# Attention and gated MLP on one core: another way to store the softmax sums, another planner model, another set of priorities

## The chip, the cores and the metric

The kernel runs on one core of a Trainium2 chip. The metric is the device time in microseconds (us) of one execution. TensorE multiplies matrices, VectorE (DVE in the profile), ScalarE (ACT) and GpSimd (POOL) work on elements, and SyncE (SP) does nothing but issue the transfers (DMAs) in the order in which the program lists them.

## The reference

For 8 batches and 8 heads, with 576 positions and 64 columns a head, in float32:

```python
q_rot, k_rot = (rotate(q), rotate(k))                 # rotary embedding
scores = np.matmul(q_rot, k_rot.transpose(0, 1, 3, 2)) / np.sqrt(D)
attn = np.exp(scores - np.max(scores, axis=-1, keepdims=True))
attn = attn / (np.sum(attn, axis=-1, keepdims=True) + 1e-09)
x = np.matmul(attn, v)                                # heads joined: B, 576, 512
h = np.maximum(x @ w_in, 0.0)                         # 576 x 1024
u, v = (h[..., :512], h[..., 512:])
v_n = (v - mean(v)) / np.sqrt(var(v) + 1e-06)
v_s = np.einsum('ts,bsd->btd', w_spatial, v_n) + b_spatial[None, :, None]
out = (u * v_s) @ w_out
```

## The kernel before

**Tiles.** Two heads of a batch are one pair; there are 32 pairs, numbered `i`, four to a batch. Of a pair, `prepare` loads q and k (`st`, L549), turns them by the rotary table (`rope` L541, `rope_sum` L545, mostly on POOL), splits them into a high and a low part (L557 on ACT, L532 on DVE, L422 for the low parts) and copies them into the stacks that TensorE reads (`stk`, L568 to L575, ten DMAs a pair). `scores` (L782) makes nine score tiles of 128 x 576; `soften` takes the row maximum (L825, DVE), the exponential with its row sums (L828, ACT) and, from the fifth pair on, a 32 x 32 block transposition (L830, DVE). The product with the values, the "v product" (L741), comes in two halves of 144 matmuls each in the profile; each half is 288 instructions with its weight loads. The first four pairs (`i < PLAIN`) take another path, with transpositions on TensorE (L664, L667) and wider v products (L710).

**The sums.** `normalise` turns the nine columns of row sums into reciprocals (L862), transposes the 128 x 32 tile in 32 x 32 blocks (`rt`, L863), so that in each of the four 32-partition groups ("quadrants") the rows hold the sums of 32 positions, and stores them to DRAM: `put`, eight DMAs for the first four pairs, six for the others. `get` reads them back, spread over 64 partitions for each head (`rb`, two DMAs), L867 multiplies, and L419 and L422 split the product `x` into its parts for the MLP.

**The MLP** of a batch (`mlp`) needs the four `x` of the batch. Its products, in order: `rows` (L901, the only ones 512 columns wide, here called wide products), u (L924), the spatial ones (L942) and the output (L957), all the last three 288 columns wide. The weights come as pairs of 32-bit words and are decoded on DVE, ACT and POOL (`decode`) in the early part of the run.

**The order.** The kernel's instructions are not issued in the order of the text. Each piece of work is an `Op` with a modelled duration, a priority (`key`, a due time worked out from the pair's number and the constants `K_...`, `DEC_...`) and its dependences. `Program.run` simulates the five engines and the DMA queue with heaps: whenever an engine is free in the model, the ready op with the smallest key that finds its buffers is issued on it. The result is a fixed order for each engine; on the chip each engine follows its own in order and waits where an operand is late. For TensorE the model also has the arrival of instructions (`Feed`, L126): 256 of them come by one fetch, and an op of more than 200 instructions (only the halves of the v product) is put off while the model says that it would stall by over `STALL` ns (L267). In the model a finished op releases its followers `LATENCY` ns after its end; TensorE's own followers too, after 200 ns, though they run on the same engine.

```python
if item[2].count > 200 and item is not dense and feed.walk(now, item[2].costs[e], item[2].count, wire, False) > STALL:
```

Of the kernel before, what the change touches and what calls it, by code (L numbers as in the profile page):

```python
# [31 lines left out]
TO_PE = 104  # L32
LATE = 1244
AHEAD = 1564
BATCH, AHEAD_OF, IN_FLIGHT = 256, 32, 8
FIRST = 1100
FETCH_MIN, FETCH_END, FETCH_LANE, SLOW, STALL = 1456, 2550, 830, 1800, 187
SLOTS = {
    "stage": 3, "lk": 1, "vrep": 1, "et": 2, "x32": 1, "xg": 7, "m": 4,
    "stk": 3, "small": 3, "nmx": 3, "rt": 2, "sc": 2, "pm": 4, "eh": 6,  # L40
# [3 lines left out]
DEC_V = [27.3, 49.5, 63.4, 71.3]  # L44
DEC_S = [38.0, 28.4, 82.6]
DEC_U = [67.4, 109.3, 103.5, 96.2]
DEC_O = [126.8, 108.3, 154.4, 146.7]
# [14 lines left out]
VALUES_AT2 = [17.2, 29.1]  # L62
K_HI, K_MUL, K_HALF = 0.94, 2.63, 5.44
# [11 lines left out]
K_TAIL = -17.27  # L75
K_INV, K_GET, K_X, K_XHI, K_XLO = 20.09, 69.48, 32.23, 48.57, 37.32
K_NORM, K_RELU, K_GATE, K_GHI, K_GLO, K_OB, K_OUT = 0.84, -5.79, -15.46, 19.4, -3.72, 0.16, 33.12
# [41 lines left out]
class Op:  # L119
    def __init__(self, costs, key, f, new, port):  # L120
        self.costs, self.key, self.f, self.new, self.port = costs, key, f, new, port
        self.eng, self.late, self.reserve, self.count = None, 0, False, 0
        self.waits, self.after, self.bufs = 0, [], []
# [27 lines left out]
class Program:  # L151
# [32 lines left out]
    def run(self, make):  # L184
# [45 lines left out]
        wire, feed, lands = 0, Feed(), [0] * IN_FLIGHT  # L230
# [4 lines left out]
        while events:  # L235
            now = events[0][0]
            while events and events[0][0] == now:
                _, _, what, o = heapq.heappop(events)
                if what == "ready":
                    for n_e, e in enumerate(o.costs):  # L240
                        heapq.heappush(ready[e], (o.key + STEAL * n_e, index[o], o))
                elif what == "free":
# [3 lines left out]
                else:  # L246
# [6 lines left out]
                    for a in o.after:  # L253
                        a.waits -= 1
                        if not a.waits:
                            late = TO_PE if PE in a.costs and o.eng != PE else 0
                            heapq.heappush(events, (now + late, n, "ready", a))
                            n += 1
            for e in LATENCY:
# [3 lines left out]
                while (ready[e] or dense) and not chosen:  # L263
# [25 lines left out]
                if chosen:  # L289
# [18 lines left out]
                    else:  # L308
                        gap = chosen.costs[e]
                        if e == PE:  # L310
                            gap += feed.walk(now, gap, chosen.count, wire, True)
                            end = now + gap
                    heapq.heappush(events, (now + gap, n, "free", e))
                    heapq.heappush(events, (end + LATENCY[e] + chosen.late, n + 1, "done", chosen))
                    n += 2
# [5 lines left out]
def tile_attention_gated_mlp(  # L321
# [21 lines left out]
    def T(shape, dt, name):  # L343
        return sb.tile(shape, dt, tag=name, name=name, bufs=1)

    def make(b):
# [6 lines left out]
        if b.pool == "rt":  # L353
            b.scratch = dr.tile([2, 5, P], F32, tag=tag, name=b.name + "d", bufs=1)
# [19 lines left out]
    sums = [T([P, 32], F32, f"sums{i}") for i in range(2)]  # L374
    wsp = T([P, 4, 2, S], F32R, "wsp")
# [141 lines left out]
    def prepare(i):  # L517
# [46 lines left out]
        for a in range(2):  # L564
# [3 lines left out]
            for dst, rows, part, tok, dep in (  # L568
# [6 lines left out]
                op(DMA, dma_ns(132, 1, 570, 2.9), key - (K_STACK2 if a else K_STACK), copy, r=[dep], w=[tok])  # L575
# [144 lines left out]
    def attention(i):  # L720
# [24 lines left out]
        o = op(PE, 2600, key + K_AV, lambda: multiply(0, half), r=need, w=pv, new=pv, count=32 * half)  # L745
        o.reserve = True
        op(PE, 2600, key + K_AV, lambda: multiply(half, NB), r=need, w=pv, count=32 * half)
# [84 lines left out]
    def normalise(i, sm, x32, key):  # L832
        rt = Buf("rt", [P, 32], F32, f"rt{i}")
# [4 lines left out]

        def put():
            main = rt.scratch[:, :4, :]  # L840
            for j in range(4):
                load(main[:, :, 32 * j:32 * j + 32], rt[32 * j:32 * j + 8, :])
            ends = rt.scratch[:, 4, :64]
            if i < PLAIN:
                for h in range(2):
                    for j in range(2):
                        load(ends[h:h + 1, 32 * j:32 * j + 32], rt[64 * h + 32 * j + 8:64 * h + 32 * j + 9, :])
            else:
                for h in range(2):
                    load(ends[h].rearrange("(g k) -> g k", g=4), rt.tile.rearrange("(g r) n -> g r n", r=32)[:, 8, 16 * h:16 * h + 16])  # L850

        def get():
            for h in range(2):
                row = rt.scratch[h].rearrange("t p -> (t p)").rearrange("(o n) -> o n", o=1)
                load(rb[64 * h:64 * h + 64, :], row[:, :S].to_broadcast([64, S]))
# [7 lines left out]
        op(DVE, 125, key + K_INV, lambda: nc.vector.transpose(out=rt.tile, in_=sm), r=need, w=[rt], new=[rt])  # L863
        op(DMA, dma_ns(5, 8 if i < PLAIN else 6, 330, 120), key + K_INV, put, r=[rt], w=[(rt, 1)])
        op(DMA, dma_ns(288, 2, 590, 5.2), key + K_GET, get, r=[(rt, 1)], w=[rb, "rbs"], new=[rb])
# [6 lines left out]
    def mlp(b):  # L872
# [6 lines left out]
        def mm(ns, f, each=HALF, **kw):  # L879
            key = base + MOE_LENGTH * spent[0] / whole  # L880
            spent[0] += ns
            op(PE, ns, key, f, count=2 * round(ns / pe_ns(each)), **kw)
# [220 lines left out]
```

## Time and profile before

| | |
|---|---|
| median of 3 runs | 846.47 us (839.14, 846.47, 847.57) |
| profiled execution | 843.61 us, of which the span from first to last instruction is 841.8 us |
| TensorE busy | 807.4 us, 96% of the span |
| DVE, ACT, POOL busy | 586.9, 527.2, 527.4 us |
| mean granted TensorE clock | 0.996 of full speed |
| DMA issues on SP | 778 |

In the profile PE is TensorE's matmuls and PEld its weight loads. An idle time is put down to the instruction whose semaphore came last; "issue" stands where the engine waited for nothing that the profile shows. The ends of matmuls are modelled, so that time in which they run slowly counts as busy.

### The profile page before, as it was taken

The page shows a single profiled execution, that of the slowest core. Times are in us where ns is not written, and L with a number is a line of the kernel's source. Part 1 is how long each engine was busy: PE and PEld are TensorE (multiplying, and loading weights), DVE is VectorE, ACT ScalarE, POOL GpSimd, SP SyncE. Part 2 cuts the span into 40 slices and gives each one's busy share as a digit, 9 for nine tenths or more (in the row PEclk, how much of TensorE's full clock was granted, in tenths as well). Part 3 has the DMA queues.
Part 4 walks back from the last instruction along what each step waited for, and adds up shares of the span by engine and source line. Part 5 has one row for each costly group of instructions (what it writes and reads, how often), then busy time and mean ns, then how long its engine had stood idle before and what let it go on. Part 6 is the DMA issues. An engine that isn't in the chain of part 4 may idle for free.

```text
span 841.8 us, 30199 instructions
## 1 busy us (share of the span) xinstructions
PE 807.4 (96%) x12560; PEld 725.6 (86%) x12560; DVE 586.9 (70%) x1172; ACT 527.2 (63%) x1378; POOL 527.4 (63%) x441
## 2 busy tenths in 40 slices
PE   5999889999999999999999999999999989999998
PEld 3556678998999988998888989998899988999898
DVE  6988987866987667676875678666587766765220
ACT  4889767565865558465764568655595555744442
POOL 5999587675758758486764758575566865423221
PEclk9999999999999999999999999999999999999999
DMA  9855666678777884778657688777757887373101
GB/s 330 295 176 139 164 177 150 176 184 218 174 188 199 193 226 131 167 182 244 168 143 190 168 198 202 180 187 187 196 145 175 216 209 178 73 166 76 44 2 57
DMA packets 63867, 144.56 MB, mean 172 GB/s; under 512 B 10993, under 2 KB 12785, under 8 KB 63730
## 3 DMA queue, kind: packets, MB, share of 16 engines
q1 hardware_dynamic: 63730, 142.63, 65.4%
q8 instruction: 99, 1.62, 0.8%
q14 instruction: 38, 0.31, 0.1%
HBM read 93.55 MB, written 9.58 MB: 123 GB/s over the span
## 4 chain that ended last, share of the span: by engine, by line
PE 75%; POOL 5%; DMA 5%; ACT 5%; DVE 4%; issue 3%; SPq 3%; POOLq 0%; DVEq 0%; ACTq 0%
PE psum L741 14%; PE psum L782 13%; PE psum L942 13%; PE psum L901 11%; PE psum L924 10%; PE psum L957 8%; SPq L416 3%; ACT et L828 2%; PE psum L802 2%; POOL st L541 2%; PE psum L710 1%; DMA st<-in_qk_dram 1%; DVE nmx L825 1%; POOL st L545 1%; PE psum L664 1%
## 5 line engine op out<-in xcount | busy, mean ns | idle before, releaser
L828 ACT ACTIVATE et<-psum,nmx 128x576 f32<-128x576 f32 x288 | 212.5, 740 | 125.4 <-DVE nmx L825 123.9
L825 DVE TENSOR_REDUCE nmx<-psum 128x1 f32<-128x576 f32 x288 | 210.7, 742 | 85.1 <-PE psum L782 77.4
L830 DVE STREAM_TRANSPOSE et<-et 128x576 f32<-128x576 f32 x252 | 192.4, 769 | 50.7 <-ACT et L828 49.6
L541 POOL TENSOR_TENSOR st<-st,tabs 128x576 f32<-128x576 f32 x112 | 164.2, 1479 | 59.1 <-DMA st<-in_qk_dram 33.5
L741 PE MATMUL psum<-et,vr 32*64 32x144 f32 x8064 | 147.0, 286 | 6.8 <-issue 2.9
L741 PEld LDWEIGHTS psum<-et,vr 32*64 32x64 f32 x8064 | 128.9, 130 | 21.8 <-issue 15.0
L942 PE MATMUL psum<-wsp,vn 128*128 128x288 f32 x768 | 124.9, 296 | 0.9 <-issue 0.9
L924 PE MATMUL psum<-x,wi 128*128 128x288 f32 x768 | 118.5, 296 | 2.4 <-issue 1.4
L901 PE MATMUL psum<-wi,x 128*128 128x512 f32 x448 | 118.6, 402 | 0.3 <-DVE sgwo L466 0.2
L957 PE MATMUL psum<-g,wo 128*128 128x288 f32 x768 | 118.2, 298 | 0.3 <-POOL g L422 0.2
L924 PEld LDWEIGHTS psum<-x,wi 128*128 128x128 f32 x768 | 108.0, 188 | 6.0 <-issue 4.0
L942 PEld LDWEIGHTS psum<-wsp,vn 128*128 128x128 f32 x768 | 109.4, 188 | 2.5 <-issue 1.6
L957 PEld LDWEIGHTS psum<-g,wo 128*128 128x128 f32 x768 | 107.5, 189 | 2.3 <-issue 1.4
L782 PE MATMUL psum<-stk 128*128 128x288 f32 x448 | 100.5, 306 | 6.7 <-ACT et L828 4.8
L422 POOL TENSOR_TENSOR g<-u,g 128x288 fp32r<-128x288 f32 x64 | 52.0, 814 | 77.8 <-ACT g L419 77.6
L782 PE MATMUL psum<-stk,stk 128*128 128x288 f32 x448 | 96.4, 297 | 0.8 <-issue 0.8
L901 PEld LDWEIGHTS psum<-wi,x 128*128 128x128 f32 x448 | 81.1, 191 | 17.6 <-issue 2.0
L782 PEld LDWEIGHTS psum<-stk 128*128 128x128 f32 x448 | 72.8, 189 | 19.1 <-ACT et L828 8.8
L422 POOL TENSOR_TENSOR vn<-vv,vn 128x512 fp32r<-128x512 f32 x32 | 42.6, 1334 | 68.5 <-ACT vn L419 66.5
L545 POOL TENSOR_TENSOR st<-st 128x576 f32<-128x576 f32 x56 | 81.1, 1449 | 2.4
L782 PEld LDWEIGHTS psum<-stk,stk 128*128 128x128 f32 x448 | 72.2, 189 | 1.0 <-issue 1.0
L422 POOL TENSOR_TENSOR x<-x,x 128x576 fp32r<-128x576 f32 x64 | 55.2, 883 | 18.0 <-ACT x L419 17.8
(133 smaller groups left out, 1005.4 us busy)
## 6 DMA issues: line engine op xcount, KB each, us to landing
vr<-in_v_dram SPq DMA_DIRECT2D x116, 320.0 KB
st<-in_qk_dram SPq DMA_DIRECT2D x62, 576.0 KB
stk<-lk SPq DMA_DIRECT2D x168, 144.0 KB
stk<-st SPq DMA_DIRECT2D x112, 128.0 KB
out_dram<-ob SPq DMA_DIRECT2D x31, 288.0 KB
ws<-in_w_spT_dram SPq DMA_DIRECT2D x2, 576.0 KB
st<-in_qk_dram SPq DMA_DIRECT2D x2, 288.0 KB
tabs<-in_tab_dram SPq DMA_DIRECT2D x2, 288.0 KB
```

The lines of the kernel that those rows point to most:

```text
L422: eng.tensor_tensor(out=lo, in0=src, in1=hi.bitcast(F32), op=ALU.subtract)
L541: f = lambda e: e.tensor_tensor(out=st[j][:, cols], in0=st[j][:, cols], in1=tabs[:, cols], op=ALU.mult)
L545: f = lambda e: e.tensor_tensor(out=st[j][:, :S], in0=st[j][:, :S], in1=st[j][:, S:2 * S], op=ALU.add)
L741: nc.tensor.matmul(bank(g)[64 * h:64 * h + 64, EACH // 9 * (1 - h):EACH // 9 * (1 - h) + EACH], lhsT=vr[rows, b % 4, b // 4, h, :], rhs=e[ ...
L782: nc.tensor.matmul(pt[:, c * 512:c * 512 + HALF], lhsT=lhsT, rhs=rhs[:, c * HALF:(c + 1) * HALF], start=(n == 0), stop=(n == len(parts) - 1))
L825: op(DVE, 680, key + K_MAX, lambda: nc.vector.tensor_reduce(out=nmx.tile, in_=tops(), op=ALU.max, axis=AX.XY, negate=True), r=[pt], w=[nmx ...
L828: op(ACT, 750, key + K_EXP, lambda: nc.scalar.activation(weights(), tops(turn), AF.Exp, bias=nmx.tile, scale=1.0, accum_out=sm[:, to:to + ...
L830: op(DVE, 705, key + K_TURN, lambda: nc.vector.transpose(out=blocks(et, at), in_=blocks(et, at)), w=[(et, at)])
L901: nc.tensor.matmul(pm.tile, lhsT=lhsT, rhs=win[1, d][:, j, :], start=(d == 0 and n == 0), stop=(d == 3 and n == len(todo) - 1))
L924: nc.tensor.matmul(pm[:, :HALF], lhsT=win[0, d][:, i, f * P:(f + 1) * P], rhs=x[d][:, at:at + HALF], start=(d == 0 and n == 0), stop=(d == ...
L942: nc.tensor.matmul(pm[:, :HALF], lhsT=lhsT, rhs=rhs, start=(t == 0 and n == 0), stop=(t == 4 and n == 1))
L957: nc.tensor.matmul(pm[:, :HALF], lhsT=wout[d,][:, i, m * P:(m + 1) * P], rhs=gs[d][:, at:at + HALF], start=(d == 0 and n == 0), stop=(d == ...
```

## The change

It has two parts that alter the instructions, and the rest alters the order in which they are issued.

- **Sums.** A persistent 128 x 128 tile `recips` takes the place of the `rt` tiles. Four DVE transpositions of 32 x 32 (`turn`) bring the sums of all four quadrants side by side into one quadrant, so that one row holds a whole 128 positions. `put` is then three DMAs: one for each head, of four rows of 512 bytes, and one for the last 64 positions of both heads. `get` is as before, from another DRAM tile.
- **Planner, TensorE to itself.** A new event `next`, at the end of an op on TensorE, releases the followers that run on TensorE at once, not 200 ns later. `TO_PE` goes from 104 to 50.
- **Planner, v products and wide products.** An op of `rows` is marked `wide`. While the last op issued on TensorE is wide, a half of the v product is reckoned to stall 310 ns more (`AFTER_WIDE`). `STALL` goes from 187 to 97, `FETCH_MIN` from 1456 to 1613; a half is reckoned at 2680 ns, not 2600.
- **Planner, others.** An ACT op that follows one on POOL becomes ready 267 ns later (`FROM_POOL`, for keys over 60), the stack copies land 399 ns later (`LATE_STACK`) and cost 620 ns of issue each, not 570; `put` is reckoned as 3 issues of 620, not 6 or 8 of 330.
- **Priorities.** Nearly all of the `K_...` and `DEC_...` constants have new values.

```diff
-TO_PE = 104
-LATE = 1244
-AHEAD = 1564
+TO_PE = 50
+LATE = 1160
+AHEAD = 1776
...
-FETCH_MIN, FETCH_END, FETCH_LANE, SLOW, STALL = 1456, 2550, 830, 1800, 187
+AFTER_WIDE = 310
+FIRST, FROM_POOL, LATE_STACK = 1100, 267, 399
+FETCH_MIN, FETCH_END, FETCH_LANE, SLOW, STALL = 1613, 2550, 830, 1800, 97
...
-STEAL = 4.21
+STEAL = 3.43
...
-K_MAX, K_EXP, K_TURN, K_AV, K_COPY = 1.21, 5.53, 2.78, 15.98, -11.29
-K_LOAD, K_ROPE, K_SUM, K_HIQ, K_LOQ, K_LOK, K_STACK, K_STACK2 = 31.39, 4.1, 26.56, -16.27, 8.05, 18.38, 13.2, 26.74
+K_MAX, K_EXP, K_TURN, K_AV, K_COPY = 2.09, 4.44, 1.66, 20.19, -15.04
+K_LOAD, K_ROPE, K_SUM, K_HIQ, K_LOQ, K_LOK, K_STACK, K_STACK2 = 26.19, 5.52, 27.16, -29.01, 11.4, 18.34, 15.25, 33.34
...
+                elif what == "next":
+                    for a in o.after:
+                        if PE in a.costs:
+                            a.waits -= 1
...
                     for a in o.after:
+                        if o.eng == PE and PE in a.costs:
+                            continue
                         a.waits -= 1
                         if not a.waits:
-                            late = TO_PE if PE in a.costs and o.eng != PE else 0
+                            late = TO_PE if PE in a.costs and o.eng != PE else FROM_POOL if ACT in a.costs and o.eng == POOL and o.key > 60 else 0
...
-                    if item[2].count > 200 and item is not dense and feed.walk(now, item[2].costs[e], item[2].count, wire, False) > STALL:
+                    if item[2].count > 200 and item is not dense and feed.walk(now, item[2].costs[e], item[2].count, wire, False) + AFTER_WIDE * wide > STALL:
...
-                op(DMA, dma_ns(132, 1, 570, 2.9), key - (K_STACK2 if a else K_STACK), copy, r=[dep], w=[tok])
+                op(DMA, dma_ns(132, 1, 620, 2.9), key - (K_STACK2 if a else K_STACK), copy, r=[dep], w=[tok]).late = LATE_STACK
...
+        def turn():
+            for j in range(4):
+                nc.vector.transpose(out=rows[:, 32 * j:32 * j + 32], in_=sm[32 * j:32 * j + 32, :])
+
         def put():
-            main = rt.scratch[:, :4, :]
-            for j in range(4):
-                load(main[:, :, 32 * j:32 * j + 32], rt[32 * j:32 * j + 8, :])
-            ends = rt.scratch[:, 4, :64]
+            for h in range(2):
+                load(scale[h, :4 * P].rearrange("(t n) -> t n", n=P), rows[4 * h:4 * h + 4, :])
+            ends, last = rows[8:9, :], scale[:, 4 * P:]
             if i < PLAIN:
-                for h in range(2):
-                    for j in range(2):
-                        load(ends[h:h + 1, 32 * j:32 * j + 32], rt[64 * h + 32 * j + 8:64 * h + 32 * j + 9, :])
+                load(last.unsqueeze(0), ends.rearrange("o (h n) -> o h n", h=2))
             else:
-                for h in range(2):
-                    load(ends[h].rearrange("(g k) -> g k", g=4), rt.tile.rearrange("(g r) n -> g r n", r=32)[:, 8, 16 * h:16 * h + 16])
+                load(last.rearrange("h (g n) -> g h n", g=4).unsqueeze(0), ends.rearrange("o (g h n) -> o g h n", g=4, h=2))
...
-        op(DVE, 125, key + K_INV, lambda: nc.vector.transpose(out=rt.tile, in_=sm), r=need, w=[rt], new=[rt])
-        op(DMA, dma_ns(5, 8 if i < PLAIN else 6, 330, 120), key + K_INV, put, r=[rt], w=[(rt, 1)])
+        op(DVE, 500, key + K_INV, turn, r=need, w=[("recips", i % 2)])
+        op(DMA, dma_ns(5, 3, 620, 60), key + K_INV, put, r=[("recips", i % 2)], w=[("scales", i % 2)])
```

## Rows read from the trace of the kernel before

**Rows 1.** The page's first part: busy time of an engine, its share of the span and its instructions.

```profile
PE 807.4 (96%) x12560; PEld 725.6 (86%) x12560; DVE 586.9 (70%) x1172; ACT 527.2 (63%) x1378; POOL 527.4 (63%) x441
```

**Rows 2.** The page's fourth part, the chain of work that ended last, by engine as shares of the span.

```profile
PE 75%; POOL 5%; DMA 5%; ACT 5%; DVE 4%; issue 3%; SPq 3%; POOLq 0%; DVEq 0%; ACTq 0%
```

**Rows 3.** The waits of PE over the whole run: who waited for whom, us in total, times, the longest. The last line is from the same view of SP.

```profile
PE psum L802 <- DVE st L614: 7.6, 1, 7.6
PE psum L782 <- ACT et L828: 6.8, 7, 2.4
PE psum L741 <- issue: 2.9, 4, 1.2
...
PE psum L782 <- DMA rt4d<-rt: 1.8, 1, 1.8
...
PE psum L741 <- ACT vv L975: 1.2, 1, 1.2
...
SPq L416 <- DVE rt L863: 22.9, 8, 13.6
```

**Rows 4.** The busy time of the engines in stretches of the run. The columns: the stretch, its length, busy us of PE, PEld, DVE, ACT and POOL with their instructions, the granted TensorE clock, the busy share of the DMA engines, GB/s.

```profile
20.00:40.00 20.00, 18.71 (x143) 11.40 (x141) 18.03 (x30) 16.64 (x43) 19.86 (x16) 1.00 0.85 291
...
100.00:120.00 20.00, 16.83 (x346) 13.92 (x346) 17.63 (x43) 12.97 (x31) 14.42 (x12) 1.00 0.83 219
...
585.00:590.00 5.00, 3.13 (x24) 2.90 (x23) 2.45 (x4) 2.73 (x7) 4.92 (x5) 1.00 1.07 217
590.00:595.00 5.00, 5.00 (x25) 4.82 (x24) 3.67 (x6) 3.42 (x10) 4.92 (x5) 0.66 0.83 243
...
690.00:695.00 5.00, 3.81 (x13) 3.18 (x14) 3.83 (x5) 3.20 (x9) 4.14 (x4) 0.75 0.88 258
```

**Rows 5.** The timeline of SP around three places: start us, length in us, the instructions. "rt...d<-rt" are the stores of the sums, "st<-in_qk_dram" the loads of q and k.

```profile
102.82 3.69 SPq L416 DMA_DIRECT2D rt4d<-rt  x6
106.61 0.38 SPq L416 DMA_DIRECT2D st<-in_qk_dram  x1
...
573.52 3.73 SPq L416 DMA_DIRECT2D rt23d<-rt  x6
577.29 0.92 SPq L416 DMA_DIRECT2D st<-in_qk_dram  x2
...
672.01 3.74 SPq L416 DMA_DIRECT2D rt27d<-rt  x6
675.80 0.92 SPq L416 DMA_DIRECT2D st<-in_qk_dram  x2
```

**Rows 6.** The timelines of POOL, ACT and PE behind the last two of these places, with the idle time before an instruction and its releaser in brackets.

```profile
583.97 2.82 POOL L541 TENSOR_TENSOR st<-st,tabs 128x576 f32<-128x576 f32 x2 [7.65 <-DMA rb<-rt23d]
...
588.32 0.68 ACT L557 ACTIVATE st<-st 128x576 fp32r<-128x576 f32 x1 [2.27 <-POOL st L545]
...
586.95 0.95 PE L957 MATMUL psum<-g,wo 128*128 128x288 f32 x6
589.77 0.61 PE L782 MATMUL psum<-stk 128*128 128x288 f32 x2 [1.87 <-ACT et L828]
...
590.66 1.65 PE L957 MATMUL psum<-g,wo 128*128 128x288 f32 x6
...
681.87 2.83 POOL L541 TENSOR_TENSOR st<-st,tabs 128x576 f32<-128x576 f32 x2 [6.30 <-DMA st<-in_qk_dram]
...
691.19 0.53 PE L782 MATMUL psum<-stk 128*128 128x288 f32 x2 [2.35 <-ACT et L828]
...
691.82 6.61 PE L901 MATMUL psum<-wi,x 128*128 128x512 f32 x21
```

**Rows 7.** The stores and the loads back of the sums of pair 0 and pair 23 (all instructions on one tile): count, then the time on SP in ns, least, median and most, and the first and last start.

```profile
L416 SPq DMA_DIRECT2D rt0d<-rt x8: 212/496/744, 21.2 to 25.4; - x8
...
L416 SPq DMA_DIRECT2D rt23d<-rt x6: 504/567/684, 573.5 to 576.7; - x6
```

**Rows 8.** The v product on PE. First its group over the whole run (busy us, mean ns of one, idle us before them and their releasers), then pieces of the timeline: two halves that follow wide products, with the wide products before them, and two slow halves.

```profile
L741 PE MATMUL psum<-et,vr 32*64 32x144 f32 x8064 | 147.0, 286 | 6.8 <-issue 2.9 <-ACT et L828 1.9 <-ACT vv L975 1.2
...
198.74 2.22 PE L901 MATMUL psum<-wi,x 128*128 128x512 f32 x9
200.88 2.51 PE L741 MATMUL psum<-et,vr 32*64 32x144 f32 x144
...
204.91 2.67 PE L741 MATMUL psum<-et,vr 32*64 32x144 f32 x144
...
449.86 2.42 PE L741 MATMUL psum<-et,vr 32*64 32x144 f32 x131
453.15 0.50 PE L741 MATMUL psum<-et,vr 32*64 32x144 f32 x13 [0.88 <-issue]
...
455.37 1.94 PE L741 MATMUL psum<-et,vr 32*64 32x144 f32 x102
458.46 0.99 PE L741 MATMUL psum<-et,vr 32*64 32x144 f32 x42 [1.15 <-issue]
```

**Rows 9.** The page's third part, DMA queues: packets, MB, share of the 16 engines; the queue that carries instructions.

```profile
q8 instruction: 99, 1.62, 0.8%
```

**Rows 10.** Small operations of DVE, grouped by line: count, busy us, mean ns of one, idle us before them.

```profile
L863 DVE STREAM_TRANSPOSE rt<-sums 128x32 f32<-128x32 f32 x32 | 6.3, 198 | 0.2
...
L981 DVE TENSOR_SCALAR sm<-sm 128x1 f32<-128x1 f32 (+1 forms) x40 | 5.5, 139 | 0.5
```

More of the change, by code (lines that the diff above doesn't have):

```diff
@@ L43 @@
 MOE_START, MOE_LENGTH = 90.55, 84.31
[L44 to L47, printed above, removed]
+DEC_V = [32.1, 52.4, 68.6, 69.1]
+DEC_S = [44.0, 28.3, 76.8]
+DEC_U = [62.5, 115.1, 99.8, 96.2]
+DEC_O = [133.5, 106.3, 156.5, 145.3]
 GATE_U = [2, 2, 3, 3]
@@ L61 @@
 KT_STEP2 = [2.4, 0.3]
-VALUES_AT2 = [17.2, 29.1]
-K_HI, K_MUL, K_HALF = 0.94, 2.63, 5.44
+VALUES_AT2 = [17.3, 29.1]
+K_HI, K_MUL, K_HALF = 1.36, 2.99, 7.32
 WHOLE = 4
@@ L229, in run @@
         held = dict.fromkeys(LATENCY, False)
-        wire, feed, lands = 0, Feed(), [0] * IN_FLIGHT
+        wire, feed, lands, wide = 0, Feed(), [0] * IN_FLIGHT, False
         events = [(0, n, "ready", o) for n, o in enumerate(self.ops) if not o.waits]
@@ L241, in run @@
                         heapq.heappush(ready[e], (o.key + STEAL * n_e, index[o], o))
+                elif what == "next":
+                    for a in o.after:
+                        if PE in a.costs:
+                            a.waits -= 1
+                            if not a.waits:
+                                heapq.heappush(events, (now, n, "ready", a))
+                                n += 1
                 elif what == "free":
@@ L310, in run @@
                         if e == PE:
+                            gap += AFTER_WIDE * (wide and chosen.count > 200)
+                            wide = chosen.wide
                             gap += feed.walk(now, gap, chosen.count, wire, True)
                             end = now + gap
+                            heapq.heappush(events, (end, n + 2, "next", chosen))
                     heapq.heappush(events, (now + gap, n, "free", e))
                     heapq.heappush(events, (end + LATENCY[e] + chosen.late, n + 1, "done", chosen))
-                    n += 2
+                    n += 3
         assert not left, "instructions wait for each other"
@@ L374, in tile_attention_gated_mlp @@
     sums = [T([P, 32], F32, f"sums{i}") for i in range(2)]
+    recips = T([P, P], F32, "recips")
+    scales = [dr.tile([2, S], F32, tag=f"scales{i}", name=f"scales{i}", bufs=1) for i in range(2)]
     wsp = T([P, 4, 2, S], F32R, "wsp")
@@ L744, in attention @@
         half = NB // 2
-        o = op(PE, 2600, key + K_AV, lambda: multiply(0, half), r=need, w=pv, new=pv, count=32 * half)
+        o = op(PE, 2680, key + K_AV, lambda: multiply(0, half), r=need, w=pv, new=pv, count=32 * half)
         o.reserve = True
-        op(PE, 2600, key + K_AV, lambda: multiply(half, NB), r=need, w=pv, count=32 * half)
+        op(PE, 2680, key + K_AV, lambda: multiply(half, NB), r=need, w=pv, count=32 * half)
         def copy(n, one):
@@ L832, in normalise @@
     def normalise(i, sm, x32, key):
-        rt = Buf("rt", [P, 32], F32, f"rt{i}")
+        rows = recips[32 * (i % 2):32 * (i % 2) + 32, :]
+        scale = scales[i % 2]
         rb = Buf("m", [P, S], F32, f"rb{i}")
@@ L881, in mm @@
             spent[0] += ns
-            op(PE, ns, key, f, count=2 * round(ns / pe_ns(each)), **kw)
+            op(PE, ns, key, f, count=2 * round(ns / pe_ns(each)), **kw).wide = each == HF
             return key
```

18 lines of the change are left out of this document (7 added, 11 removed).

## The prediction

> **What bounds the kernel now.** I read the page's busy times first. TensorE is busy 807.4 us of the 841.8 us span, and no other engine is over 586.9 [rows 1]. The change leaves TensorE's 12560 matmuls as they are, so it can gain only three things: time in which TensorE is idle, 34.4 us by these rows; time in which it is busy but slow; and nothing else. The chain of work that ended last names TensorE for 75% only [rows 2], but most of the other quarter runs beside TensorE's work and is not for the taking; the 34.4 us are the better bound.
>
> Next I read what TensorE waited for [rows 3]. The largest single wait, 7.6 us, is the start of the run: the first scores wait for the first q and k. Some 3 us more lie behind the last matmul, where the output leaves. The change touches neither. That leaves about 34.4 - 7.6 - 3.2 = 23.6 us of idle time, in about thirty waits of 2.4 us or less. The longest group is scores (L782) held up by the exponentials (L828), 6.8 us in seven waits. To see why, I went to the two longest, at 588 and 689 us, and followed them back through the timelines. They are the same event. SP issues the six stores of a pair's sums, which takes it 3.73 and 3.74 us, and only then the loads of q and k for a later pair [rows 5]. POOL sits idle for 7.65 and 6.30 us and then starts on q and k; ACT stands behind POOL with its high part (at 588 for 2.27 us), the exponentials stand behind that on ACT, their score buffers stay taken, and TensorE is idle for 1.87 and 2.35 us [rows 6]. So the sums, which nobody needs soon, hold up a load that somebody does need. [...] Six products of L957 take 1.65 us there and 0.95 us just before, and 21 wide products take 6.61 us [rows 6], where nine take 2.22 us at full speed [rows 8], so that 21 would take 5.2.
>
> The third thing is the v product. Its 56 halves (28 pairs) are busy 147.0 us, with 6.8 us of idle time before or inside them. An undisturbed half takes 2.51 us [rows 8]; 56 of them are 140.6, so 147.0 + 6.8 - 140.6 = 13.2 us are lost there. About 3.1 of these are waits for ACT [rows 8]; the other 10.1 are waits put down to "issue" and slow passages, as at 450 and 455 us, where two halves take 3.8 and 4.1 us with holes of 0.88 and 1.15 us [rows 8].
>
> **The change part by part.** All sums are against the profiled execution, 843.61 us.
>
> Sums, stores. Six DMAs of a median 567 ns, or eight of 496, become three [rows 7]. I price a new one like an old one: 3 x 0.57 to 0.62 = 1.7 to 1.9 us in place of 3.7, so SP is free about 1.9 us earlier in each pair; 104 issues fewer, some 60 us of SP in all. Nearly all of it is hidden beside TensorE. What is not hidden are the places of rows 5. Against the 1.9 us stand the added transpositions: four of 32 x 32 in place of one of 128 x 32. No row shows one of that size; the nearest are the old one, 198 ns, and a 128 x 1 operation, 139 ns [rows 10], so four cost 0.56 to 0.79 us, 0.36 to 0.59 more than now. I take 0.5. The store waits for all four; SP already waits 22.9 us behind such a store for DVE [rows 3], and whatever is queued behind it on SP (loads of q and k, stack copies) waits too. Net 1.4 us earlier. At 588 and 689 us that takes 1.4 us off each wait: **-2.8**. What is left, 0.5 and 0.95 us, I reckon too short for the clock to fall, because waits of 1.2 and 1.8 us lie between 100 and 120 us, at a full clock [rows 3, 4]. The clock's price is 1.65 - 0.95 = 0.7 us on L957 and about as much again on the score products around it, say 1.6, and 6.61 - 5.2 = 1.4 at 692 us: **-3.0**, with 0 as the other end. A third place is at 103 us: TensorE waits 1.8 us with a store of sums as the last releaser [rows 3], six stores on SP [rows 5]; **-1.3**, other end 0.
>
> Sums, DVE. 32 x 0.36 to 0.59 = 12 to 19 us more busy time. DVE has 841.8 - 586.9 = 255 us free [rows 1], so this is hidden, except in the first 100 us, where DVE and POOL pace the run (18.03 and 19.86 us of 20 busy [rows 4]). Four pairs lie there: 4 x 0.5 = 2 us if nothing covers it, 0 if all; I take **+1.0**.
>
> v products, the fetch. A longer modelled fetch and a lower `STALL` make the plan put a half off until its instructions are in. It speaks to the 10.1 us. The plan already does so and still loses them, so I take about a third, **-3.5**; the ends are 0 and -10.1. The rows: the instruction queue moved 99 packets and 1.62 MB [rows 9], 16.4 KB each, and the holes fall inside the halves, where instructions are used up fastest. [...]
>
> v products, away from wide products. The two rows behind wide products take 2.51 and 2.67 us [rows 8]: clean, the best places there are. Moving a dozen halves elsewhere costs 12 x 0.16 = 1.9 us at the most if they fall where a half is as clean as the worse of these, and gains as much the other way; I take **+0.5**. If they fall on places like 450 us it is more; that is the third rival.
>
> TensorE to itself at once. In the model a product's next step may follow directly, so that more runs of one kind stay together. No row shows a price for a change from one kind of product to another, so I give the new grouping none; **0**, between -2 and +2 (the length of one of the waits above) through when buffers come free. With it the second half of a v product may follow the first directly.
>
> `FROM_POOL`, `LATE_STACK`, priorities. They move ACT's and SP's waits; the chain at 588 us is just that case (ACT behind POOL), and the gain is counted above. The other waits, some 6 us of 1 us each, belong to no one edit: a new order removes some and makes others. I take **0**, with -6 and +6 as ends.
>
> Sum: -2.8 - 3.0 - 1.3 + 1.0 - 3.5 + 0.5 = -9.1, so 843.61 - 9.1 = 834.5 for a run like the profiled one. The median of the runs before stands 2.9 us above the profile, and the runs spread from 839.1 to 847.6; the median after then lies between 834.5 and 837.4. I give 836.
>
> **The rivals.** [...]
>
> (2) *Much more goes.* The plan now knows what the chip does: half of the 23.6 us, two thirds of the 10.1 us, and all of the clock's 3: 11.8 + 6.7 + 3.0 = 21, so 822, or 825 as a median. For it: the old plan reckons a store at 330 ns where the profile has 567 [rows 7], so its idea of SP was off by 1.4 us a pair. Against it: the old plan was already wrong in few places.
>
> (3) *Slower: the second halves meet an empty queue.* With "at once" and away from the wide products, the second half comes right behind the first, 576 instructions with nothing slow between, and runs like the one at 455 us: 4.1 against 2.5 us [rows 8], 1.6 us each. If half of the 28 do, that is +22; with the sums' gains, 843.6 + 22 - 7 = 859. It decides from about six such halves (6 x 1.6 = 9.6 cancels the forecast). Against it: `STALL` at 97 is there to prevent just this, if the model of the fetch is right.
>
> **How the numbers follow.** The measurement tells about 1% from no change; 1% of 846.47 puts the limits at 838 and 855. Chances: the forecast (832 to 839) 0.40; rival 1 (839 to 850) 0.31; rival 2 (820 to 832) 0.16; rival 3 (over 850, mostly over 855) 0.13. Faster by over 1% is rival 2 and most of the forecast, 0.16 + 0.35 = 0.51; slower by over 1% is 0.12; the rest, 0.37, is within. For 8 in 10, the range keeps the forecast and rival 1, and half of rival 2: 826 to 850.
>
> **What would show it in the profile after.** SP: 32 x 3 stores, some 1.8 us a pair, and 674 issues in all. DVE: four small transpositions a pair at 140 to 200 ns, busy about 600 us. PE: the two waits of about 2 us at the ends of batches under 1 us, and no stretch with a granted clock under 0.9 after the start. v products: the group's busy and idle time together near 150 us, not 154, and few halves directly behind L901. [...] What would make the forecast wrong is mostly the new priorities: they reach every engine, and I price them at nothing.

## The result and the profile after

The changed kernel took 845.02 us (median of 20 runs, 842.57 to 853.95), the kernel before 840.59 us in 20 runs beside them (836.78 to 848.37). The ratio is 1.006, with a 95% interval of 1.0033 to 1.0087: 0.6% or about 5 us slower, where I had forecast 9 us less than the profiled run. The two profiled executions show nothing of it: 843.37 us after, 843.61 us before. The profile of before happened to stand 3 us over its kernel's median, that of after 1.7 us under its own.

The first part of the page and the waits of TensorE, to be read against [rows 1] and [rows 3]:

```profile
PE 803.4 (96%) x12560; PEld 724.5 (86%) x12560; DVE 614.9 (73%) x1268; ACT 534.4 (64%) x1378; POOL 522.7 (62%) x441
```

```profile
PE psum L815 <- DVE st L627: 7.4, 1, 7.4
PE psum L795 <- ACT et L841: 6.8, 14, 1.2
PE psum L677 <- DVE turns L688: 6.2, 2, 5.7
...
PE psum L754 <- issue: 1.9, 4, 1.0
```

(L795 is the old L782, the scores; L754 the old L741, the v product; L815 the old L802; L677 the old L664.) TensorE is busy 4.0 us less and idle 37.2 us (840.6 - 803.4) instead of 34.4. The group that I wanted to shorten, scores behind the exponentials, has no wait of 2 us any more, but fourteen small ones in place of seven, and the same sum, 6.8 us. And there is a new wait, 5.67 us long. It stands in the early part, and two stretches of the run show it (columns as in [rows 4]):

```profile
40.00:60.00 20.00, 14.17 (x83) 8.22 (x83) 17.57 (x24) 10.74 (x26) 15.71 (x14) 0.80 0.40 136
60.00:80.00 20.00, 19.10 (x140) 11.64 (x138) 17.11 (x31) 18.80 (x48) 13.61 (x11) 0.95 0.44 132
```

The timelines of DVE, POOL and PE there, in this order:

```profile
46.89 6.32 DVE L470 TENSOR_SCALAR sgwi<-wi13raw 128x512 int32<-128x512 int32 x1
53.13 1.41 DVE L838 TENSOR_REDUCE nmx<-psum 128x1 f32<-128x576 f32 x2
```

```profile
46.11 1.37 POOL L400 MEMSET stk<- 64x576 f32 x2
47.45 1.40 POOL L641 TENSOR_TENSOR st<-st,tabs 128x576 f32<-128x576 f32 x1
48.83 1.39 POOL L554 TENSOR_TENSOR st<-st,tabs 128x576 f32<-128x576 f32 x1
50.18 1.39 POOL L642 TENSOR_TENSOR st<-st 128x576 f32<-128x576 f32 x1
51.53 1.39 POOL L554 TENSOR_TENSOR st<-st,tabs 128x576 f32<-128x576 f32 x1
52.89 1.57 POOL L435 TENSOR_TENSOR wt<-wst,wt 64x576 fp32r<-64x576 f32 x1
```

```profile
55.66 0.90 PE L677 MATMUL psum<-turns,et 128*128 128x128 f32 x3 [5.67 <-DVE turns L688]
```

One decode operation of DVE (L470, weights `wi13`) takes 6.32 us while POOL, without a gap, ends its second memset and runs four more operations; it ends 0.32 us into the next one. Everything on DVE stands behind it, TensorE waits 5.67 us, and the granted clock is 0.80 in this stretch, 0.50 from 52 to 60 us. Other parts of the change do what they were made for:

```profile
L754 PE MATMUL psum<-et,vr 32*64 32x144 f32 x8064 | 144.1, 285 | 5.2 <-ACT et L841 3.0 <-issue 1.9
...
L855 DVE STREAM_TRANSPOSE recips<-sums 32x32 f32<-32x32 f32 x128 | 25.6, 200 | 2.0
```

```profile
43.15 1.26 SPq L429 DMA_DIRECT2D scales<-recips  x3
```

The first line is the v product of [rows 8], 149.3 us with its idle time instead of 153.8; the second the new transpositions, 200 ns each; the third the stores of one pair, 1.26 us instead of the 3.7 of [rows 5].

### The profile page after: what moved, and what is told of

The parts are those of the page before. It is cut to its first block, busy times and chain, and to the rows that moved or that the text cites. A ratio compares the mean times of both kernels' runs of the same rounds, so it can differ in the third digit from the quotient of the medians.

```text
span 840.6 us, 30171 instructions
## 1 busy us (share of the span) xinstructions
PE 803.4 (96%) x12560; PEld 724.5 (86%) x12560; DVE 614.9 (73%) x1268; ACT 534.4 (64%) x1378; POOL 522.7 (62%) x441
## 4 chain that ended last, share of the span: by engine, by line
PE 75%; DMA 6%; DVE 6%; ACT 5%; POOL 4%; issue 3%; SPq 1%; DVEq 0%; POOLq 0%; ACTq 0%
PE psum L754 14%; PE psum L795 14%; PE psum L955 13%; PE psum L937 10%; PE psum L914 10%; PE psum L970 9%; ACT et L841 3%; DMA st<-in_qk_dram 2%; DVE nmx L838 2%; PE psum L815 2%; DMA vr<-in_v_dram 2%; PE psum L677 1%; POOL st L554 1%; PE psum L723 1%; DMA rb<-scales 1%
## 5 line engine op out<-in xcount | busy, mean ns | idle before, releaser
L554 POOL TENSOR_TENSOR st<-st,tabs 128x576 f32<-128x576 f32 x112 | 161.0, 1452 | 29.6 <-DMA st<-in_qk_dram 23.3
L754 PE MATMUL psum<-et,vr 32*64 32x144 f32 x8064 | 144.1, 285 | 5.2 <-ACT et L841 3.0
L754 PEld LDWEIGHTS psum<-et,vr 32*64 32x64 f32 x8064 | 126.8, 130 | 16.6 <-issue 11.9
L955 PE MATMUL psum<-wsp,vn 128*128 128x288 f32 x768 | 120.1, 295 | 0.0
L937 PE MATMUL psum<-x,wi 128*128 128x288 f32 x768 | 114.3, 296 | 1.4 <-DVE x L772 1.2
L970 PE MATMUL psum<-g,wo 128*128 128x288 f32 x768 | 113.9, 297 | 0.1
L914 PE MATMUL psum<-wi,x 128*128 128x512 f32 x448 | 112.2, 397 | 0.5 <-ACT ob L973 0.5
L937 PEld LDWEIGHTS psum<-x,wi 128*128 128x128 f32 x768 | 106.2, 188 | 3.1 <-DVE x L772 1.5
L970 PEld LDWEIGHTS psum<-g,wo 128*128 128x128 f32 x768 | 105.5, 188 | 2.3 <-issue 2.0
L795 PE MATMUL psum<-stk 128*128 128x288 f32 x448 | 100.2, 305 | 7.0 <-ACT et L841 5.5
L795 PE MATMUL psum<-stk,stk 128*128 128x288 f32 x448 | 95.5, 295 | 0.0
L795 PEld LDWEIGHTS psum<-stk 128*128 128x128 f32 x448 | 72.4, 188 | 19.8 <-ACT et L841 10.0
L435 POOL TENSOR_TENSOR lk<-st,lk 128x576 fp32r<-128x576 f32 x28 | 40.2, 1437 | 65.9 <-ACT lk L432 41.5
L795 PEld LDWEIGHTS psum<-stk,stk 128*128 128x128 f32 x448 | 71.6, 188 | 0.0
```

Source lines behind the costliest of these rows:

```text
L435: eng.tensor_tensor(out=lo, in0=src, in1=hi.bitcast(F32), op=ALU.subtract)
L554: f = lambda e: e.tensor_tensor(out=st[j][:, cols], in0=st[j][:, cols], in1=tabs[:, cols], op=ALU.mult)
L754: nc.tensor.matmul(bank(g)[64 * h:64 * h + 64, EACH // 9 * (1 - h):EACH // 9 * (1 - h) + EACH], lhsT=vr[rows, b % 4, b // 4, h, :], rhs=e[ ...
L795: nc.tensor.matmul(pt[:, c * 512:c * 512 + HALF], lhsT=lhsT, rhs=rhs[:, c * HALF:(c + 1) * HALF], start=(n == 0), stop=(n == len(parts) - 1))
L914: nc.tensor.matmul(pm.tile, lhsT=lhsT, rhs=win[1, d][:, j, :], start=(d == 0 and n == 0), stop=(d == 3 and n == len(todo) - 1))
L937: nc.tensor.matmul(pm[:, :HALF], lhsT=win[0, d][:, i, f * P:(f + 1) * P], rhs=x[d][:, at:at + HALF], start=(d == 0 and n == 0), stop=(d == ...
```

## The experiments

To take the parts apart, the order of issue that a planner finds was recorded and then replayed instruction by instruction with the other kind of sums. "Old order" is that of the kernel before, "new order" that of the changed one. Ratios are to the kernel before, run beside them. All waits are TensorE's, where nothing else is said.

**The kernel before, once more.** No edit.

> The kernel before, unchanged, for a second trace. If the two waits that the prediction priced (1.87 us at 588 us and 2.35 us at 689 us, each with a slow clock behind it) belong to this order of instructions, they stand in this trace too, within 0.5 us. If they belong to the one execution that was profiled (843.6 us, where the median of 20 runs is 840.6), at least one of them is under 1 us here, and the granted clock of 580 to 600 and 680 to 700 us is over 0.95.

845.0 us. TensorE at the two places of [rows 6]:

```profile
594.87 0.53 PE L782 MATMUL psum<-stk 128*128 128x288 f32 x2 [0.60 <-ACT et L828]
...
693.35 0.53 PE L782 MATMUL psum<-stk 128*128 128x288 f32 x2 [1.65 <-ACT et L828]
```

The same places, but 0.60 and 1.65 us in place of 1.87 and 2.35, and the mean clock is 1.000. The sizes at these places and the slow clock belonged to the one execution that I had priced. The kind of wait did come again, at a third place:

```profile
298.83 0.53 PE L782 MATMUL psum<-lk,qt 128*128 128x288 f32 x2 [2.64 <-ACT et L828]
```

Its chain is the same: six stores of sums take SP 3.72 us at 277.85 us, POOL then is idle for 3.51 us until a load of q and k lands, and ACT stands behind POOL for 2.29 us. The whole group makes 7.7 us, against 6.8 in [rows 3]. Yet behind this wait of 2.64 us the clock stays full (1.00 from 300 to 305 us).

**New sums in the old order.** `turn`, the three stores and `get` of the change; the order untouched.

> The order of the kernel before on every engine, with the new sums alone: four small transpositions and three stores a pair. Theory of the prediction (the stores hold up the loads behind them on SP): 2 to 6 us faster than before, ratio 0.993 to 0.998, and the waits of about 2 us at 588 and 689 us at least 1 us shorter. Rival (hidden): ratio 0.998 to 1.002. Rival (the new sums are what costs the time, through DVE or through slower stores): ratio 1.004 or more.

846.92 us, ratio 1.0075 [1.0046, 1.0103]. The waits at 588 and 689 us are gone, and the sums still cost 6 us. Two lines of the waits (L743 and L784 are the old L741 and L782):

```profile
PE psum L743 <- issue: 7.9, 6, 2.6
PE psum L784 <- ACT et L830: 3.6, 8, 1.2
```

The waits for the exponentials went down, those put down to "issue" went up (11.7 us in all, from 5.9 and 7.1 in the two executions of the kernel before).

**Old sums in the new order.** One 128 x 32 transposition and six or eight stores, everything else as changed.

> The order of the changed kernel on every engine, with the old sums: one transposition and eight or six stores a pair. If the new sums gain, this is slower than the changed kernel (1.006 of before): ratio to before 1.009 to 1.014. If they are hidden: 1.004 to 1.008. If they are what costs: 1.002 or less. In each case the wait of TensorE of 5.7 us at about 50 us should still be there if it belongs to the order.

837.38 us, ratio 0.9964 [0.9932, 0.9996]. The v product, and the stretch from 40 to 60 us:

```profile
L754 PE MATMUL psum<-et,vr 32*64 32x144 f32 x8064 | 144.0, 285 | 5.5 <-ACT et L841 3.0 <-issue 1.4 <-ACT vv L988 0.9
```

```profile
40.00:60.00 20.00, 19.61 (x144) 11.74 (x145) 16.88 (x29) 17.91 (x45) 19.31 (x16) 1.00 0.55 170
```

So the planner's half of the change is a small gain, just clear of the noise, and the sums are a loss on either order. What remained was which half of the sums, and what the 6.32 us are.

**A wait on POOL that keeps the collision away.** In the changed kernel one operation of a single column was added on POOL, right behind the decode step; it reads that step's output:

```diff
+        if n == "wi13":
+            o.then = lambda: nc.gpsimd.tensor_tensor(out=gate1, in0=sg[:, :1].bitcast(F32), in1=sg[:, :1].bitcast(F32), op=ALU.add)
```

> The changed kernel in its own order, with one 128x1 addition more on POOL that reads the result of the DVE operation which took 6.32 us at 46.9 us (the first step of decoding the fourth weight tile for v). POOL so stops once until that operation is done. Theory (the operation could not start beside POOL's unbroken work): it takes under 1.5 us, TensorE's wait of 5.7 us at 50 us falls under 1 us, the clock stays full from 40 to 80 us, and the whole is 7 to 10 us faster than the changed kernel: ratio to before 0.994 to 0.998. Rival (the operation waited for its data or for DVE itself): it still takes 5 us or more, POOL now waits as well, ratio 1.006 or more.

839.67 us, ratio 1.0002 [0.997, 1.0034], where the changed kernel has 1.006: about 5 us less. DVE, POOL and PE at the place:

```profile
46.95 0.88 DVE L473 TENSOR_SCALAR sgwi<-wi13raw 128x512 int32<-128x512 int32 x1
```

```profile
46.17 1.37 POOL L403 MEMSET stk<- 64x576 f32 x2
47.97 0.19 POOL L479 TENSOR_TENSOR gate<-sgwi 128x1 f32<-128x1 f32 x1 [0.43 <-DVE sgwi L473]
48.11 1.41 POOL L646 TENSOR_TENSOR st<-st,tabs 128x576 f32<-128x576 f32 x1
```

```profile
50.26 0.55 PE L682 MATMUL psum<-turns,et 128*128 128x128 f32 x3 [0.21 <-DVE turns L693]
```

POOL stops for 0.43 us, the decode step takes 0.88 us, TensorE's wait is 0.21 us, and the clock stays full there. All that came as the theory has it; the gain is less than the 7 to 10 us that I expected.

**The changed kernel, once more.** No edit; is the collision a property of the order?

> The changed kernel itself, a second time, for its trace. Theory (the collision belongs to the order, not to one execution): the decode of wi13 on VectorE near 47 us takes over 4 us again, beside GpSimd work without a gap, TensorE is idle for over 4 us at about 55 us with the copies of the transpositions as the releaser, and the granted clock of 40 to 60 us is under 0.9; time 843 to 848. Rival (it belongs to the one execution, and the 5 us that the wait on GpSimd gave back came from elsewhere): that operation takes under 1.5 us, no wait over 2 us stands between 45 and 65 us, and the time is either near 840 or lost at other places after 100 us.

843.84 us. It is there again, to the hundredth:

```profile
46.96 6.32 DVE L470 TENSOR_SCALAR sgwi<-wi13raw 128x512 int32<-128x512 int32 x1
```

```profile
55.73 0.90 PE L677 MATMUL psum<-turns,et 128*128 128x128 f32 x3 [5.67 <-DVE turns L688]
```

**The transpositions alone, old order.** Old stores; three idle 32 x 32 transpositions are added in front of the old one.

```diff
+            for j in range(1, 4):
+                nc.vector.transpose(out=rt[0:32, :], in_=sm[32 * j:32 * j + 32, :])
             nc.vector.transpose(out=rt.tile, in_=sm)
```

> The order of the kernel before and its old stores, with three more 32x32 transpositions on DVE in each pair (their result is not used): the DVE share of the new sums alone. The new sums as a whole made this order slower by 0.75%. If DVE's added 0.6 us a pair is what costs: ratio 1.004 to 1.010. If the stores cost it: 1.002 or less.

847.91 us, ratio 1.0107 [1.006, 1.0153]. DVE's group, then TensorE's waits (L929 is the old L924), and last the wait behind `sm` in the kernel before:

```profile
L841 DVE STREAM_TRANSPOSE rt<-sums 32x32 f32<-32x32 f32 x96 | 19.2, 200 | 3.2
```

```profile
PE psum L929 <- DVE sm L991: 2.4, 1, 2.4
...
PE psum L741 <- ACT vv L980: 2.0, 1, 2.0
PE psum L667 <- DVE turns L675: 1.8, 2, 1.1
```

```profile
PE psum L924 <- DVE sm L986: 1.1, 1, 1.1
```

19.2 us more on DVE cost 9 us (1.07% of 840.4; 5 to 13 by the interval, from six runs). The wait behind DVE at 127 us was 1.1 us before, and the one behind ACT at 104 us 1.2 us [rows 3]. Counted by TensorE's work done, this execution loses 4.3 us between 20 and 176 us against both profiled ones of the kernel before; at the end it is 5.7 and 7.1 us behind. The run with the new sums in this order loses 5.5 us in the same stretch, with waits of 1.1, 2.0 and 2.3 us at the same three places. The run with the stores alone, below, loses 0.6 us there. So this part of the loss goes with the transpositions. DVE is nearly full there (columns as in [rows 4]):

```profile
80.00:100.00 20.00, 18.57 (x139) 13.52 (x138) 19.61 (x35) 19.13 (x53) 15.31 (x13) 1.00 0.41 116
100.00:120.00 20.00, 16.79 (x340) 13.52 (x339) 19.17 (x47) 12.11 (x30) 12.12 (x11) 1.00 0.86 211
```

**The transpositions alone, new order.** The same edit on the new order.

> The order of the changed kernel and the old stores, with three more 32x32 transpositions on DVE in each pair (their result is not used). Theory: the 0.6 us that they add on DVE ahead of the decoding are what makes its operation at 47 us miss the gap in POOL's work; it then takes 5 us or more, TensorE's wait of over 5 us at 50 us is back, and the ratio to before is 1.003 to 1.010 (0.9964 without the three). Rival (the stall came with the new stores): the operation takes under 1.5 us and the ratio is 0.996 to 1.001.

843.28 us, ratio 1.0022 [0.9991, 1.0053]: a loss of 0.58% against the new order with the old sums. I had expected the collision in it; it isn't there in the trace (that operation took 0.88 us at 46.39 us). This execution loses its time between 600 and 700 us, in two waits of 2.07 and 2.25 us for the exponentials. SP, POOL and PE at the first of them, and the stretch behind it:

```profile
624.29 3.71 SPq L429 DMA_DIRECT2D rt1d<-rt  x6
```

```profile
634.14 2.83 POOL L554 TENSOR_TENSOR st<-st,tabs 128x576 f32<-128x576 f32 x2 [3.80 <-DMA st<-in_qk_dram]
```

```profile
639.94 0.40 PE L795 MATMUL psum<-stk 128*128 128x288 f32 x1 [2.07 <-ACT et L841]
```

```profile
640.00:645.00 5.00, 5.00 (x26) 5.00 (x27) 4.02 (x6) 3.44 (x9) 5.00 (x6) 0.66 0.85 189
```

That is the chain that the prediction priced, six stores ahead of the loads, with the slow clock behind it; at 692 us it stands once more. The trace of this order with the old sums alone has neither. So the loss is measured, but this trace does not show it as work that DVE had no room for; why the chain closes here and not there is open.

**The stores alone, old order.** Three stores, one of the four transpositions; three quarters of the reciprocals are left out, a constant stands in their place.

```diff
-            for j in range(4):
+            for j in range(1):
                 nc.vector.transpose(out=rows[:, 32 * j:32 * j + 32], in_=sm[32 * j:32 * j + 32, :])
```

> The order of the kernel before with the three new stores, but one of the four small transpositions (three are left out, so that three quarters of the reciprocals are a constant): the share of the stores alone. If DVE is what costs, this shows the gain that the prediction priced: ratio 0.992 to 0.998. If the shorter stores themselves cost (loads that start earlier meet the fetch of TensorE's instructions), ratio 1.003 or more, and the waits put down to issue grow over the 7.0 us that they make in the kernel before.

843.89 us, ratio 1.003 [0.9998, 1.0062]: no gain. TensorE's waits (L744, L785, L947, L962 are the old L741, L782, L942, L957), and then two of these waits on the timeline:

```profile
PE psum L744 <- issue: 6.4, 8, 1.5
PE psum L962 <- issue: 3.5, 2, 1.9
PE psum L785 <- ACT et L831: 2.5, 6, 1.2
...
PE psum L947 <- issue: 1.6, 1, 1.6
PE psum L785 <- DMA stk<-st: 1.5, 1, 1.5
```

```profile
589.48 1.32 PE L962 MATMUL psum<-g,wo 128*128 128x288 f32 x8 [1.60 <-issue]
...
686.00 0.96 PE L962 MATMUL psum<-g,wo 128*128 128x288 f32 x6 [1.89 <-issue]
```

The mechanism of my store term worked: the waits of the scores for the exponentials fell to 2.5 us, from 6.8 in [rows 3] and 7.7 in the second run of that kernel. The waits put down to "issue" took the gain back: 12.7 us in all, from 5.9 and 7.1. Two of them stand 6 and 9 us of work ahead of the two places that I had priced, and behind the second, from 685 to 690 us, the clock is 0.69.

**The same with the old number of stores.** Three idle stores more in each pair (five in the first four pairs) fill SP up again.

```diff
+            for h in range(5 if i < PLAIN else 3):
+                load(spare[:, 6 * i + h, :], rows[4 * (h % 2):4 * (h % 2) + 4, :])
```

> The order of the kernel before, the three new stores and one transposition as in the run with the new stores alone (three quarters of the reciprocals are again a constant), and as many idle stores of 2 KB to DRAM as make the number of stores a pair that of the kernel before (three more, five for the first four pairs). Theory (freeing SP lets the loads behind start earlier and meet the fetch of TensorE's instructions): the waits put down to issue fall from 12.4 us to 9 us or less and the ratio from 1.003 towards 1.000, while the waits for the exponentials rise again from 2.5 us. Rival (the new form of the stores is slow in itself): the ratio stays at 1.003 or goes up.

842.44 us, ratio 1.0003 [0.9973, 1.0033].

```profile
PE psum L786 <- ACT et L832: 5.7, 9, 1.5
PE psum L745 <- issue: 3.7, 4, 2.4
```

Both go back: 5.7 us behind the exponentials, 8.1 us of "issue" in all. The two are traded against each other, and the time hardly moves (the intervals of the two runs overlap). All executions in the old order side by side, us waited in the whole run, with the waits for DVE at the very start left out:

| | for exponentials | "issue" | for DVE | ratio |
|---|---|---|---|---|
| before, two executions | 10.6, 10.6 | 5.9, 7.1 | 1.6, 1.7 | 1 |
| stores alone | 7.6 | 12.7 | 1.4 | 1.003 |
| the same, old number of stores | 9.1 | 8.1 | 1.3 | 1.0003 |
| transpositions alone | 12.2 | 5.7 | 5.0 | 1.0107 |
| new sums | 6.8 | 11.7 | 4.4 | 1.0075 |

**Two edits of the planner.** On the new order with the old sums, `AFTER_WIDE` at 60 instead of 310, and the event `next` taken out, each with its newly planned order.

```diff
-AFTER_WIDE = 310
+AFTER_WIDE = 60
```

> The planner and the priorities of the changed kernel with the old sums, and AFTER_WIDE 60 in place of 310, which makes a new order: 5 halves of the v product stand behind wide products, where none did. If staying off the wide products is worth 310 ns a half, these 5 halves take about 0.3 us more each than undisturbed ones (2.75 against 2.44 us from start to start); theory: they take 2.44 to 2.6 us as in the kernel before, and the edit has no price of its own. Time to before 0.990 to 1.006, since every new order moves some waits.

847.32 us, ratio 1.0078 [1.0049, 1.0108].

```diff
-                elif what == "next":
-                    for a in o.after:
...
-                        if o.eng == PE and PE in a.costs:
-                            continue
...
-                            heapq.heappush(events, (end, n + 2, "next", chosen))
```

> The planner and the priorities of the changed kernel with the old sums, but TensorE's own followers wait 200 ns in the model again (the event next is taken out): a new order. If that edit carries the gain of the new order (0.9964 with the old sums), the ratio is 1.000 or more and the waits put down to issue are back at 5 us or more; if it has no price of its own, the ratio lies within 0.004 of 0.9964.

867.54 us, ratio 1.0339 [1.0274, 1.0403]. DVE there:

```profile
49.85 5.24 DVE L460 TENSOR_SCALAR sgwi<-wi13raw 128x512 int32<-128x512 int32 x1
```

Both are worse than the order that they stem from (837.38). In the first the thing edited has no price that shows: of the five halves behind wide products four take 2.44 to 2.52 us and one 2.92 us. The second shows the signs that I had set for "the event carries the gain": a ratio over 1.000 and 9.1 us of "issue", from 1.9. But that is 7 of the 30 us that it lost; much of the rest stands in longer waits for the exponentials, for stack copies and for ACT, and one decode step takes 5.24 us (2.94 us in the first run). Both edits threw the whole order. So these runs do not say what an edit of the planner is worth.

**Fewer stores without more transpositions.** New order, old transposition; the two stores of the last 64 positions become one from the fifth pair on, five in place of six.

```diff
-                for h in range(2):
-                    load(ends[h].rearrange("(g k) -> g k", g=4), rt.rearrange("(g r) n -> g r n", r=32)[:, 8, 16 * h:16 * h + 16])
+                load(ends.rearrange("h (g k) -> g h k", g=4), rt.rearrange("(g r) (h k) -> g r h k", r=32, h=2)[:, 8, :, :])
```

> The order of the changed kernel, the one old transposition, and five stores in place of six from the fifth pair on (the last 64 positions of both heads in one). If a shorter SP part is worth anything in this order: ratio 0.993 to 0.996; if it is hidden, 0.9964 again within 0.002.

835.93 us, ratio 0.993 [0.9895, 0.9964]: faster than both kernels. Against the new order with all six stores (0.9964 [0.9932, 0.9996]) the intervals overlap, so the store's own gain is not shown.

## Why the prediction was wrong

**The two long waits, -2.8, and the slow clock, -3.0.** The chain SP, POOL, ACT, exponentials was right: shorter stores alone brought this group from about 7 us to 2.5. The size was wrong. I took it from one execution; the next one has 0.60 us at the first place, a wait of 2.64 us at another, and a mean clock of 1.000, where I had priced 0.66 and 0.75 over 5 us [rows 4]. Nor does the length of a wait tell the clock: it stayed full behind that 2.64 us and fell to 0.69 behind 1.89 us in the run with the stores alone. And the gain didn't stay: with the shorter stores came about 6 us more of "issue" waits, two of them shortly ahead of the places priced. I had weighed the "issue" waits only for the v products, never as a price of freeing SP. Stores alone gave +0.3% [-0.02, +0.62], where these two terms and the next made -0.8%. That the three stores are even shorter than I priced (1.26 us, not 1.7 to 1.9) did not help.

**The wait at 103 us, -1.3.** It is 1.53 us with the new stores alone, behind a stack copy, and 1.92 us behind the same kind of copy in the second run of the kernel before. The store was only the last of several to come.

**DVE, +1.0.** This is the step that failed most. The price of one operation was nearly right: 0.60 us a pair, forecast 0.36 to 0.59. The words "DVE has 255 us free, so this is hidden" were not. The transpositions alone cost 9 us in the old order and 5 in the new one, where their one trace does not show the loss on DVE. I used a mean over the run where the stage decides: of the old order's loss 4.3 us lie between 20 and 176 us, and from 20 to 140 us DVE is busy 17.7 to 19.6 of 20 us in five of six stretches; for the early part I had priced 2 us at most. In the changed kernel TensorE waits 9.0 and 8.8 us for DVE (two traces, the start left out), and 0.8 us in the same order with the old sums: some 8 us more, of which 5 are the collision below.

**The v products, -3.5 and +0.5.** The size was right. They take 4.5 us less with their idle time (forecast 3.0), and "issue" in the whole run is 2.1 and 3.3 us in the two traces of the changed kernel. In the two executions before, 8 and 12 such waits stand beside 99 packets of the instruction queue [rows 9], and cost 5.9 and 7.1 us. None of the 56 halves follows a wide product directly now, and most take the undisturbed time (median 2.44 us from start to start), so moving them away had no visible price. The third rival's mechanism did not come: no half follows another half directly, and the slowest takes 3.8 us from its first instruction to the next product in one trace and 4.1 us in the other.

**TensorE at once, priorities, 0.** With the old sums the new order gives -0.36% [-0.68, -0.04]. That is 3 us, and the v products alone gained 4.3 us with the old sums (149.5 us), so for the rest about 0 was fair, but which edit carries what stays open.

**What I did not price.** The collision at 47 us: about 5 us in the changed kernel, as the run with the wait on POOL shows. By TensorE's work done, the changed kernel falls 8 to 9 us behind there in its two traces, against the second profiled execution of the kernel before, and gains 9 to 11 us on it from there to the end; so the profile, read only by its totals, looked like no change. It belongs to neither half alone: it is absent in the trace of the new order with the old sums (0.88 us for that operation), absent with only the transpositions added, and there with both. The first line here is from the changed kernel, the others from the new order with the old sums:

```profile
46.13 0.84 DVE L470 TENSOR_SCALAR sgwi<-wi12raw 128x512 int32<-128x512 int32 x1
```

```profile
45.46 0.42 DVE L470 TENSOR_SCALAR sgwi<-wi12raw 128x512 int32<-128x512 int32 x1
45.79 0.88 DVE L470 TENSOR_SCALAR sgwi<-wi13raw 128x512 int32<-128x512 int32 x1
```

```profile
45.56 1.63 POOL L400 MEMSET stk<- 64x576 f32 x2
```

Both traces with the collision have the decode step before it (`wi12`) 0.02 us behind the start of POOL's memsets. The three of this order without it, old sums, transpositions added, five stores, have it 0.09 to 0.14 us ahead. So a tenth of a microsecond goes with 5 us; that it decides is not shown. My own closing words, that the priorities reach every engine and are priced at nothing, pointed at the order but gave no mechanism; a slower end was left to a rival of another kind.

**The sum.** The time lies between 839 and 850 us, to which the prediction gave 0.31, the first rival's share. Waits changed their owner, and the v products gained 4.5 us; what cancelled such gains was a cost: on DVE in both orders, and in the old order in "issue" waits too. The footing was wrong as well. I took the kernel's median to stand 2.9 us above the profiled run, from three runs; over 20 runs it stands 3.0 us below. That 845.02 lies inside my range of 826 to 850 us is luck: laid on 840.59, the range would be some 6 us lower. New order -0.36%, new sums about +1% on it, and 1.006 is the result. Taking the collision away leaves 1.0002, some 0.4% above the old sums, with overlapping intervals, so that this rest is not clear of the noise. The transpositions alone (+0.58%) can bear it; that these shares simply add is not shown.

## What to carry to other kernels

An engine's free time counts only in the stage where the work is added (19.2 us more on DVE, with 255 us free, cost 9 us here); price small operations by the stretch in which that engine paces the run. Take a wait from at least two executions before pricing it, and for each queue that is freed look at the other waits too ("issue" went from 5.9 and 7.1 to 12.7 us here). When an order is fixed ahead, look in the trace for single operations many times longer than their group's mean: one such meeting cost 5 us here, more than the 3 us that the new order had gained.

## What the runs showed of the hardware

- A SBUF to SBUF tensor-scalar operation of DVE, 128 x 512 int32, that takes 0.41 to 0.88 us for the same weights in other traces took 6.32 us (twice) and 5.24 us. Where it took 6.32 us POOL ran back to back, over the rest of a memset and four more instructions; in the run in which POOL stopped there for 0.43 us it took 0.88 us. All three times it ended 0.32 us after the start of a POOL operation on `wt`. What keeps it from ending earlier no run shows.
- A 32 x 32 transposition takes 200 ns on DVE, as long as the 128 x 32 one of [rows 10]: four quadrants cost four times as much.
- The three stores, two of them with rows of 512 bytes, take SP 0.43 us each as a mean, where six with pieces of 128 bytes or less took 0.62 us each [rows 5].
- The waits put down to "issue" stand at one place in every 256 of TensorE's instructions, the number that the planner takes for one fetch. Counted along these instructions (matmuls, weight loads and some 170 others, about 25,290 in a trace), each of the 108 such waits in the 14 traces stands where the count leaves 193 or 194 when divided by 256. The 25,290 make 98.8 times 256, beside 99 packets of the instruction queue [rows 9] and 98 after the change; so a wait for the next block of instructions fits, but no trace shows which packet a wait stands for.
- These waits went from 5.9 and 7.1 to 12.7 us with no change in TensorE's matmuls or their order, and came to 8.1 us when idle stores were added. That earlier transfers lengthen them is my reading of this; what they wait for was not measured.
